# Moving the shifted bit pattern of some VectorE exponential groups to GpSimd, in seven pieces each

## The chip, the cores and the metric

The kernel runs on one core of one Trainium2 chip. The metric is the device time of one launch in microseconds (us). The engines are called by the names of the profile: PE is TensorE (matmuls; PEld are its weight loads), ACT is ScalarE, DVE is VectorE, POOL is GpSimd, and SP issues the DMAs. In the profile L1227 means line 1227 of the kernel.

## The reference

A layer norm of `x` (2048 tokens of 512 features) feeds two branches, whose results are added to `x`: an attention of 32 heads of 16 features each, and a gated linear unit with 1792 hidden features.

```python
qkv = (xn @ wqkv).reshape(B, S, 3, H, Dh)            # H = 32, Dh = 16
scores = jnp.einsum("bhqd,bhkd->bhqk", q, k) * (Dh ** -0.5)
p = softmax(scores)
A = jnp.einsum("bhqk,bhkd->bhqd", p, v).reshape(B, S, D) @ wo
gate, up = xn @ W_gate, xn @ W_up
Bo = (gate * (gate > 0) * up) @ W_down
return x + A + Bo
```

The softmax needs 32 x 2048 x 2048 exponentials. They are the largest part of the work outside the matmuls, and the change is in how some of them are made.

## The kernel before

**Blocks, groups, units.** The attention is cut into 32 blocks: four stretches of 512 queries (`c4`), four groups of heads (`gg`) and two halves (`ee`). A block covers four heads at a time, and has 16 groups, one for each stretch of 128 keys (`kt`). A group is four score tiles of 128 keys by 512 queries, one for each of the four heads. A score tile is a matmul at L1195 into a PSUM bank.

**Two ways to an exponential.** Most groups go to ACT, in units of three and two tiles in turn (L1262): one `Exp` activation from PSUM into a ring in SBUF. 108 groups go to DVE instead. The table `D_POS` says which positions of each block they take. There `dve_exp` builds the exponential from bit patterns. Four passes (named d1, L1211) turn a score tile in PSUM into the 16-bit pattern of a power of two, each 512 columns of the tile `tp`. From `tp` come three more tiles of 128 x 2048: `tm` (d2 at L1222 and d5, a product, at L1226), `tn` (d3, L1224) and `ts_`, which is the pattern of `tp` with the integer 36 added (d4, L1227). The sum of the four, with weights that are put into copies of V, stands for the exponential; so a DVE group has four PV matmuls for each head (L1171, `pv_group`) where an ACT group has one. The tiles `tp`, `tn`, `tm` and `ts_` lie in `dring`, a ring with `NDR` = 9 slots of 2048 columns.

**PV.** The PV matmuls of a block accumulate in one PSUM bank. Apart from the first and the last of a block their order is free (`PV_FREE`). After the last one the bank is copied out (L1105), the sums go by DMA to POOL, which forms the reciprocals (L1123), these come back by DMA, and POOL multiplies the block's output by them in four pieces (L1133).

**Other work in the same loop.** Projections, the gated linear unit and the output projection use the matmul at L728, whose results leave PSUM through DVE passes at L780, L811, L935, L939 and L976.

**What sets the order.** Nothing runs as a loop on the chip. The kernel records each operation with an engine, a planned duration, a priority and its tiles (`Graph.op`); `Graph.run` then places all of them by list scheduling, gives out buffer slots as it goes, and so fixes one order for each engine's queue; `emit` writes the queues with semaphore waits. Two rules of `run` matter here. Operations with `lock=True` on DVE and POOL are not placed on top of each other. And an operation named `pm` on POOL is placed only beside a DVE operation that isn't locked, after the DVE operation before that one has ended; that end becomes a real wait, and the piece has to fit into the host's time with at most `SLIP` = 100 ns over. The DVE operations from PSUM are not locked; d2, d3, d4 and d5 are. Before the change only the four multiplies at L1133 are named `pm`.

Of the kernel before, what the change touches and what calls it, by code (L numbers as in the profile page):

```python
# [9 lines left out]
U16 = mybir.dt.uint16  # L10
FP16 = mybir.dt.float16
ACTF = mybir.ActivationFunctionType
ALU = mybir.AluOpType
# [19 lines left out]
NWS = 3  # L33
NQ = 3
NDR = 9
KD = (1, 5, 9, 13)
D_LEAD = 10.0
D_POS = (
    (), (2, 3, 8, 11), (2, 8, 11, 15), (6, 9, 10),
    (2, 4, 12), (1, 3, 9, 14), (5, 10, 15), (2, 3, 10, 11),  # L40
    (1, 5, 15), (3, 4, 5, 8), (5, 9, 15), (2, 3, 7, 13),
    (3, 4, 10), (2, 4, 9, 11), (2, 7, 12), (4, 9, 10, 14),
    (7, 10, 11), (1, 8, 9, 10), (6, 7, 11, 12), (3, 5, 11),
    (1, 8, 12, 14), (4, 8, 14), (8, 12, 15), (2, 7, 13, 15),
    (1, 8, 14), (3, 4, 11), (1, 6, 10, 13), (1, 7, 12),
    (1, 8, 9), (1, 8, 11), (1, 2, 6, 12), (1, 2, 8, 9),
# [26 lines left out]
SHIFT = 36  # L73
# [379 lines left out]
def bass_parallel_sum__mha_block__glu_gated_reglu__prompt_kernel(  # L453
# [16 lines left out]
    with ExitStack() as es:  # L470
        def sb(name, shape, dt):
            return es.enter_context(nc.sbuf_tensor(name, shape, dt))
# [27 lines left out]
        ring = sb("ring", [128, NRING * 5, 512], BF16)  # L500
        dring = sb("dring", [128, NDR, 4 * 512], BF16)
        vd = sb("vd", [128, len(KD), 2, H, VW], BF16)
        hT = sb("hT", [128, FT, 512], BF16)
# [12 lines left out]
        G = Graph()  # L516
        P_sc = Pool("sc", 2)
        P_b = Pool("b", 3)
        P_ring = [Pool("ring%d" % i, NRING) for i in range(2)]
        P_dr = Pool("dr", NDR)  # L520
        P_xn = Pool("xn", 4)
# [18 lines left out]
             reads=[t_pid], writes=[t_pid], prio=-890)  # L540
        G.op("DVE", 100, lambda e: e.tensor_scalar(hmask[:, 1:2], pid[:, 0:1], 1.0 / 16.0, None, op0=ALU.mult),
             reads=[t_pid], writes=[t_mask], prio=-889)
        G.op("DVE", 100, lambda e: e.tensor_scalar(hmask[:, 0:1], pid[:, 0:1], -1.0 / 16.0, 1.0, op0=ALU.mult, op1=ALU.add),
             reads=[t_pid], writes=[t_mask0], prio=-888)
# [4 lines left out]
             reads=[t_id], writes=[t_id], prio=-898)  # L549
# [9 lines left out]
             reads=[t_id32], writes=[t_id32], prio=60)  # L559
# [13 lines left out]
        for i in range(2):  # L573
            dma(lambda e, i=i: e.dma_start(q_scr[i, :, DH:2 * DH, :], qT[:, 0, :]), 128,
                reads=[t_qt0], writes=[t_qz[i]], prio=-600)
# [35 lines left out]
        for j in range(4):  # L611
            for ee in range(2):
                dma(lambda e, j=j, ee=ee: e.dma_start(Wo_p[32 * j:32 * j + DH, ee, :], wo_src[NGG - 1, j, ee, :, :]), 16,
                    reads=[t_woz], writes=[Tile()], prio=40)
# [198 lines left out]
        def proj_v(kt, prio, allowed=(1,)):  # L813
# [7 lines left out]
            else:  # L821
                G.op("DVE", 610, lambda e: e.tensor_copy(v_aug[:, kt, :, 0:DH], bank_of(t).rearrange("p (h d) -> p h d", h=H)),
                     reads=[t], writes=[tv], prio=prio)
            if kt in KD:
                i = KD.index(kt)
                tvd = t_vd[kt] = Tile("vd")
# [6 lines left out]
        blocks = [(c4, gg, ee) for c4 in range(NB) for gg in range(NGG) for ee in range(2)]  # L833
        order, on_dve = [], set()
        for blk, cuts in zip(blocks, D_POS):
            kts = list(KD) if blk != blocks[0] else [13, 9]
            take = sorted(cuts)
            mine = [kt for kt in range(NT) if kt not in kts[:len(take)]]
            seq = []
# [6 lines left out]
                seq.append(kt)  # L846
            order.append(seq)
        groups = [blk + (kt,) for blk, seq in zip(blocks, order) for kt in seq]
        units, at_group, cur = [], {}, []
        for g in groups:  # L850
            at_group[g] = len(units) + 0.0
# [299 lines left out]
        def pv_group(key, kt, u):  # L1151
# [9 lines left out]
            for k in range(ways):  # L1161
# [5 lines left out]
                def pv(e, k=k):  # L1167
                    ins = None
                    for j in range(4):
                        v = v_aug[:, kt, 8 * gg + 2 * j + ee, 0:VN] if k < 2 else vd[:, KD.index(kt), k - 2, 8 * gg + 2 * j + ee, 0:VN]  # L1170
                        ins = e.matmul(ps_b[32 * j:32 * j + VN, 0, :], v, src[j][1](k), start=(first and k == 0),  # L1171
# [21 lines left out]
        def score(e, bank, t):  # L1193
            c4, gg, ee, kt, j = t
            return e.matmul(bank, kT[32 * j:32 * j + 32, gg, 128 * kt:128 * kt + 128],  # L1195
                            qm[32 * j:32 * j + 32, t_q[(c4, gg)].slot, ee, :], start=True, stop=True, tile_position=(32 * j, 0))
# [3 lines left out]
        def dve_exp(g, u):  # L1200

            tp, tm, tn, ts_ = (Tile("dr", P_dr) for _ in range(4))
            t4 = [g + (j,) for j in range(4)]
            prev_d, mine = list(last_d), []
            for j, t in enumerate(t4):
                ts = Tile("ds", P_b, D_BANKS)
                G.op("PE", 225, lambda e, t=t, ts=ts: score(e, ps_b[:, ts.slot, :], t), mode="row", rows=(j,), reads=[t_q[t[:2]], t_k[(t[1], t[3] // 4)], t_kfirst] + ([t_q1] if t[:3] == (0, 0, 1) else []), writes=[ts],
                     prio=u + D_WAIT, name="dsc", after=u - D_AHEAD, order=prev_d if D_SEQ else ())
                G.ops[-1].acq.append(tp)
                mine.append(G.ops[-1])  # L1210
                o = G.op("DVE", 610, lambda e, j=j, ts=ts: e.tensor_scalar(dring[:, tp.slot, 512 * j:512 * j + 512].bitcast(U16), ps_b[:, ts.slot, :],  # L1211
                                                                    0.25 * LOG2E * 128.0, 128.0 * (127.0 - LOG2_SUM), op0=ALU.mult, op1=ALU.add),
                         reads=[ts], writes=[tp], prio=u - 960, name="d1")
                for w in tp.w[:-1]:
                    o.deps.pop(w, None)
                if tp in o.acq:
                    o.acq.remove(tp)
            last_d[:] = mine

            def b(t, dt=BF16):  # L1220
                return dring[:, t.slot, :].bitcast(dt) if dt is not BF16 else dring[:, t.slot, :]
            G.op("DVE", 600, lambda e: e.tensor_scalar(b(tm, U16), b(tp, U16), 0xFF80, None, op0=ALU.bitwise_or),  # L1222
                 reads=[tp], writes=[tm], prio=u - 3, name="d2", lock=True)
            G.op("DVE", 600, lambda e: e.tensor_scalar(b(tn, U16), b(tp, U16), 0xFF80, 1, op0=ALU.bitwise_and, op1=ALU.bitwise_or),  # L1224
                 reads=[tp], writes=[tn], prio=u - 2.5, name="d3", lock=True)
            G.op("DVE", 1140, lambda e: e.tensor_tensor(b(tm), b(tp), b(tm, I16), ALU.mult), reads=[tm, tp], writes=[tm], prio=u - 3, name="d5", lock=True)  # L1226
            G.op("DVE", 600, lambda e: e.tensor_scalar(b(ts_, U16), b(tp, U16), float(SHIFT), None, op0=ALU.add),  # L1227
                 reads=[tp], writes=[ts_], prio=u - 2.4, name="d4", lock=True)
            for i in range(4):
                where[g + (i,)] = ((tp, tn, tm, ts_), lambda k, i=i: dring[:, (tp, tn, tm, ts_)[k].slot, 512 * i:512 * i + 512])  # L1230

# [2 lines left out]
        for u, cl in enumerate(units):  # L1234
# [5 lines left out]
            n = len(cl)  # L1240
            while dve_todo and dve_todo[0][0] <= u:
                dve_exp(dve_todo.pop(0)[1], u)
# [24 lines left out]
            while pv_next < len(groups) and all(groups[pv_next] + (j,) in where for j in range(4)):  # L1267
                g = groups[pv_next]
# [4 lines left out]
        for i in range(4):  # L1273
# [26 lines left out]
            if i not in FIN_PE:  # L1300
                G.op("DVE", 610, lambda e, i=i, to_=to_, tz=tz: e.tensor_tensor(xn_sb[:, to_.slot, :], bank_of(tz), resid(i), ALU.add),
                     reads=[tz, t_res[m]], writes=[to_], prio=NU + 10 + i)
            else:
                G.op("ACT", 600, lambda e, to_=to_, tz=tz: e.activation(xn_sb[:, to_.slot, :], bank_of(tz), ACTF.Copy),
                     reads=[tz], writes=[to_], prio=NU + 10 + i)
            dma(lambda e, m=m, to_=to_: e.dma_start(out2[128 * m:128 * (m + 1), :], xn_sb[:, to_.slot, :]), 128, reads=[to_], writes=[Tile()],
                prio=NU + 10 + i, stream=("out", m % 8))
# [50 lines left out]
```

The softmax here doesn't subtract the row's maximum and nothing guards it: scores larger than these inputs give would overflow.

## Time and profile before

The time is 770.96 us, the median of 2 runs (770.05 to 771.87). The profiled run has a span of 772.3 us. The columns below are the groups of the page: total busy time of the group and the mean of one instruction.

| what | line | engine | count | busy us | mean ns |
|---|---|---|---|---|---|
| exponentials | L1262 | ACT | 647 | 739.4 | 1259 (two shapes mixed) |
| d1, PSUM to `tp` | L1211 | DVE | 432 | 289.6 | 684 |
| d5, product | L1226 | DVE | 108 | 131.2 | 1215 |
| d2 | L1222 | DVE | 108 | 73.9 | 686 |
| d3 | L1224 | DVE | 108 | 73.8 | 684 |
| reciprocals | L1123 | POOL | 30 | 95.0 | 3166 |

The page also draws the span in 40 equal slices, where 9 means busy for 90% or more of the slice:

```profile
DVE  8799999999999899999799999999999989999996
ACT  6999999999999999999799999999999999999995
POOL 3103012221213222121220122213012212221200
PEclk9999999999999999999799999999999999999999
```

Read down a column to see which engines are full at the same time. DVE and ACT are full nearly everywhere; POOL is mostly idle. The row PEclk is the clock that TensorE was granted, in tenths of full speed.

### The profile page before, as it was taken

How to read it: one execution, taken by the hardware profiler on the slowest of the kernel's cores; microseconds unless marked ns; L12 is line 12 of the kernel's file. 1: busy time of each engine (PE TensorE's matmuls, PEld its weight loads, DVE VectorE, ACT ScalarE, POOL GpSimd, SP SyncE). 2: the span in 40 equal slices, each digit the busy share in tenths (PEclk: the TensorE clock that was granted, in tenths of full speed). 3: DMA queues.
4: the chain of work that ended last, by engine and by line, in shares of the span. 5: the costliest groups of instructions: out<-in, count | busy, mean ns of one | idle time of the engine just before them, and what ended most of it. 6: DMA issues, size and time to landing. Idle time of an engine off the chain costs nothing.

```text
span 772.3 us, 21574 instructions
## 1 busy us (share of the span) xinstructions
PE 752.1 (97%) x9478; PEld 226.4 (29%) x9478; DVE 735.8 (95%) x1148; ACT 747.7 (97%) x662; POOL 159.8 (21%) x172
## 2 busy tenths in 40 slices
PE   8999999999999999999999999999999999999997
PEld 3322222222222322222223233222222322222323
DVE  8799999999999899999799999999999989999996
ACT  6999999999999999999799999999999999999995
POOL 3103012221213222121220122213012212221200
PEclk9999999999999999999799999999999999999999
DMA  7402221212111122222221122132310122231000
GB/s 224 136 12 65 55 59 28 71 43 73 48 31 42 58 75 56 57 68 71 51 62 37 43 71 70 46 82 71 79 48 23 55 65 77 66 91 37 23 24 33
DMA packets 95757, 46.83 MB, mean 61 GB/s; under 512 B 69936, under 2 KB 91824, under 8 KB 95664
## 3 DMA queue, kind: packets, MB, share of 16 engines
q1 hardware_dynamic: 95664, 45.46, 21.6%
q8 instruction: 74, 1.21, 0.6%
q14 instruction: 19, 0.16, 0.1%
HBM read 36.70 MB, written 8.50 MB: 59 GB/s over the span
## 4 chain that ended last, share of the span: by engine, by line
DVE 52%; PE 40%; ACT 6%; issue 1%; POOL 0%; DMA 0%; DVEq 0%
DVE dring L1211 19%; PE ps_b L728 15%; PE ps_b L1171 11%; PE ps_sc L1195 11%; DVE dring L1226 8%; ACT ring L1262 6%; DVE dring L1224 5%; DVE dring L1222 4%; DVE dring L1227 4%; DVE up_sb L935 3%; PE ps_b L1195 2%; DVE hT L939 2%; DVE Wv L1105 1%; DVE kT L811 1%; DVE stats L637 1%
## 5 line engine op out<-in xcount | busy, mean ns | idle before, releaser
L1262 ACT ACTIVATE ring<-ps_sc 128x1536 bf16<-128x1536 f32 (+1 forms) x647 | 739.4, 1259 | 8.7 <-PE ps_sc L1195 3.9
L1211 DVE TENSOR_SCALAR dring<-ps_b 128x512 uint16<-128x512 f32 x432 | 289.6, 684 | 15.0 <-PE ps_b L1195 14.2
L1195 PE MATMUL ps_sc<-qm,kT 32*128 32x512 bf16 x1616 | 261.0, 386 | 3.5 <-ACT ring L1262 2.2
L1195 PE MATMUL ps_b<-qm,kT 32*128 32x512 bf16 x432 | 164.0, 387 | 1.8 <-DVE dring L1211 1.2
L1171 PE MATMUL ps_b<-ring,v_aug 128*17 128x512 bf16 x1616 | 144.5, 384 | 3.4 <-DVE Wv L1105 2.4
L1123 POOL TENSOR_TENSOR rrec<-rsum,minus 128x16 f32<-128x16 f32 x30 | 95.0, 3166 | 177.4 <-DMA rsum<-Wv 177.3
L1226 DVE TENSOR_TENSOR dring<-dring 128x2048 bf16<-128x2048 bf16 x108 | 131.2, 1215 | 0.0
L1195 PEld LDWEIGHTS ps_sc<-qm,kT 32*128 32x128 bf16 x1616 | 61.9, 91 | 229.9 <-ACT ring L1262 202.2
L1133 POOL TENSOR_TENSOR x_sb<-Wv,rb 128x128 bf16<-128x128 f32 x100 | 45.6, 456 | 334.4 <-DVE dring L1226 98.7
L1171 PE MATMUL ps_b<-dring,vd 128*17 128x512 bf16 x864 | 80.3, 384 | 1.0 <-DVE dring L1226 0.5
L1171 PE MATMUL ps_b<-dring,v_aug 128*17 128x512 bf16 x864 | 80.2, 386 | 0.1
L1222 DVE TENSOR_SCALAR dring<-dring 128x2048 uint16<-128x2048 uint16 x108 | 73.9, 686 | 0.7
L1224 DVE TENSOR_SCALAR dring<-dring 128x2048 uint16<-128x2048 uint16 x108 | 73.8, 684 | 0.0
L1227 DVE TENSOR_SCALAR dring<-dring 128x2048 uint16<-128x2048 uint16 x108 | 73.2, 684 | 0.0
L728 PE MATMUL ps_b<-xnT,wus 128*32 128x512 bf16 x896 | 70.8, 392 | 0.8 <-DVE dring L1211 0.5
L728 PE MATMUL ps_b<-xnT,wgs 128*32 128x512 bf16 x896 | 69.3, 386 | 1.3 <-DVE up_sb L935 0.3
L1171 PEld LDWEIGHTS ps_b<-ring,v_aug 128*17 128x17 bf16 x1616 | 36.9, 89 | 59.9 <-issue 35.0
L1195 PEld LDWEIGHTS ps_b<-qm,kT 32*128 32x128 bf16 x432 | 38.7, 91 | 43.9 <-DVE dring L1211 26.2
L728 PE MATMUL ps_b<-Wd,hT 128*32 128x512 bf16 x672 | 50.3, 382 | 0.0
L935 DVE COPY up_sb<-ps_b 128x512 f32<-128x512 f32 x56 | 38.3, 684 | 1.9 <-PE ps_b L728 1.9
L1171 PEld LDWEIGHTS ps_b<-dring,vd 128*17 128x17 bf16 x864 | 20.5, 89 | 34.4 <-issue 10.6
L939 DVE SCALAR_TENSOR_TENSOR hT<-ps_b,up_sb 128x512 bf16<-128x512 f32 x42 | 28.7, 683 | 1.4 <-PE ps_b L728 1.4
(109 smaller groups left out, 373.7 us busy)
## 6 DMA issues: line engine op xcount, KB each, us to landing
rb<-rec_scr SPq DMA_DIRECT2D x30, 256.0 KB
wus<-in_B_W_up_dram SPq DMA_DIRECT2D x56, 128.0 KB, 2.7
wgs<-in_B_W_gate_dram SPq DMA_DIRECT2D x56, 128.0 KB, 2.4
qm<-q_scr SPq DMA_DIRECT2D x30, 128.0 KB
o_scr<-x_sb SPq DMA_DIRECT2D x25, 128.0 KB
q_scr<-qT SPq DMA_DIRECT2D x17, 128.0 KB
xr_sb<-in_A_x_dram SPq DMA_DIRECT2D x16, 128.0 KB, 2.4
out_dram<-xn_sb SPq DMA_DIRECT2D x16, 128.0 KB, 1.7
```

The lines of the kernel that those rows point to most:

```text
L728: ins = e.matmul(bank_of(tile, sub)[32 * j:32 * j + 32, :], st[:, 32 * j:32 * j + 32], mv, start=(i == 0), stop=(i == n - 1), tile_positio ...
L935: G.op("DVE", 610, lambda e: e.tensor_copy(up_sb[:, tup.slot, :], bank_of(tu)), reads=[tu], writes=[tup], prio=slots[1] + EV)
L1123: G.op("POOL", 3000, lambda e: e.tensor_tensor(rrec[:, par, :], rsum[:, par, :], minus[:, 0:1].to_broadcast([128, 16]), ALU.pow), reads=[t ...
L1133: o = G.op("POOL", 200 + 1080 // N_MUL, lambda e, a=w * k, b=w * k + w: e.tensor_tensor(oT_of(tn)[:, a:b], o_sb[:, to.slot, a:b], rb[:, tr ...
L1171: ins = e.matmul(ps_b[32 * j:32 * j + VN, 0, :], v, src[j][1](k), start=(first and k == 0), stop=(last and k == ways - 1), tile_position=( ...
L1195: return e.matmul(bank, kT[32 * j:32 * j + 32, gg, 128 * kt:128 * kt + 128], qm[32 * j:32 * j + 32, t_q[(c4, gg)].slot, ee, :], start=True ...
L1211: o = G.op("DVE", 610, lambda e, j=j, ts=ts: e.tensor_scalar(dring[:, tp.slot, 512 * j:512 * j + 512].bitcast(U16), ps_b[:, ts.slot, :], 0 ...
L1222: G.op("DVE", 600, lambda e: e.tensor_scalar(b(tm, U16), b(tp, U16), 0xFF80, None, op0=ALU.bitwise_or), reads=[tp], writes=[tm], prio=u - ...
L1224: G.op("DVE", 600, lambda e: e.tensor_scalar(b(tn, U16), b(tp, U16), 0xFF80, 1, op0=ALU.bitwise_and, op1=ALU.bitwise_or), reads=[tp], writ ...
L1226: G.op("DVE", 1140, lambda e: e.tensor_tensor(b(tm), b(tp), b(tm, I16), ALU.mult), reads=[tm, tp], writes=[tm], prio=u - 3, name="d5", loc ...
L1227: G.op("DVE", 600, lambda e: e.tensor_scalar(b(ts_, U16), b(tp, U16), float(SHIFT), None, op0=ALU.add), reads=[tp], writes=[ts_], prio=u - ...
L1262: return e.activation(ring[:, a:a + n, :], ps_sc[:, 3 * k0:3 * k0 + n, :], ACTF.Exp, scale=0.25)
```

## The change

For some of the 108 DVE groups the tile `ts_` is no longer made by one d4 pass on DVE, but on POOL. The new table `POOL_AT` names for each block the positions whose group does so, as far as they are positions of `D_POS`. The 2048 columns are cut into `N_ADD` = 7 pieces of 292 or 293 columns. Each piece is an operation named `pm` with `lock=True`, so the planner lays it beside a DVE pass that reads PSUM. The planned duration of a piece is 100 ns and `P_NS` = 1.4 ns for each column, its priority that which d4 had. The pieces wait for one another only in the queue's order, and the tile counts as written when the last one is done. `D_POS` is as it was, so the same 108 groups are on DVE. The purpose is to free DVE of these passes and to use time in which POOL is idle.

```diff
+N_ADD = 7
+P_NS = 1.4
+P_PRIO = -2.4
+POOL_AT = ((), (2,), (), (6,), (), (1,), (), (2,), (), (3,), (), (2,), (), (2,), (), (4,), (), (1,), (), (3,), (), (4,), (), (2,), (), (3,), (), (1,), (), (1,), (), (1,))
...
         groups = [blk + (kt,) for blk, seq in zip(blocks, order) for kt in seq]
+        on_pool = {blk + (seq[i],) for n, (blk, seq, cuts) in enumerate(zip(blocks, order, D_POS)) for i in POOL_AT[n] if i in cuts}
...
-            G.op("DVE", 600, lambda e: e.tensor_scalar(b(ts_, U16), b(tp, U16), float(SHIFT), None, op0=ALU.add),
-                 reads=[tp], writes=[ts_], prio=u - 2.4, name="d4", lock=True)
+            if g in on_pool:
+                cuts = [2048 * k // N_ADD for k in range(N_ADD + 1)]
+                for a, z in zip(cuts, cuts[1:]):
+                    o = G.op("POOL", 100 + int(P_NS * (z - a)), lambda e, a=a, z=z: e.tensor_scalar(b(ts_, U16)[:, a:z], b(tp, U16)[:, a:z], float(SHIFT), None, op0=ALU.add),
+                             reads=[tp], writes=[ts_] if a == 0 else [], prio=u + P_PRIO, name="pm", lock=True)
+                    if a:
+                        o.order.add(ts_.w[0])
+                        ts_.w.append(o)
+            else:
+                G.op("DVE", 600, lambda e: e.tensor_scalar(b(ts_, U16), b(tp, U16), float(SHIFT), None, op0=ALU.add),
+                     reads=[tp], writes=[ts_], prio=u - 2.4, name="d4", lock=True)
```

## The prediction

> **What bounds the kernel now.** I read the busy shares on the page first, then the windows by stage, then the groups of instructions, the waits, and a piece of the timeline.
>
> ```profile
> PE 752.1 (97%) x9478; PEld 226.4 (29%) x9478; DVE 735.8 (95%) x1148; ACT 747.7 (97%) x662; POOL 159.8 (21%) x172
> ```
>
> Three engines stand at 95 to 97%, so the shares alone do not say which one an edit on DVE (VectorE) would have to relieve. The windows do (columns: length, then busy us of PE, PEld, DVE, ACT, POOL, then the granted clock):
>
> ```profile
> 20.00:60.00 40.00, 38.41 (x511) 12.43 (x506) 33.53 (x64) 39.18 (x37) 5.83 (x5) 1.00 0.25 75
> 60.00:350.00 290.00, 284.15 (x3532) 82.69 (x3528) 286.65 (x435) 288.51 (x254) 63.12 (x66) 1.00 0.21 55
> 350.00:400.00 50.00, 48.80 (x583) 13.63 (x579) 45.71 (x69) 45.82 (x41) 9.67 (x10) 0.90 0.25 65
> 400.00:550.00 150.00, 148.46 (x1890) 44.26 (x1890) 147.34 (x223) 149.71 (x132) 32.37 (x31) 1.00 0.23 61
> 550.00:600.00 50.00, 48.67 (x578) 13.67 (x570) 49.17 (x76) 48.84 (x45) 9.71 (x10) 0.97 0.18 44
> 600.00:755.00 155.00, 154.48 (x2053) 46.66 (x2045) 146.96 (x219) 154.25 (x136) 32.06 (x34) 1.00 0.20 54
> ```
>
> ACT (ScalarE) is busy 99.5% or more from 60 to 350, 400 to 550 and 600 to 755 us, while DVE drops to 146.96 of 155 in the last of these and to 286.65 of 290 in the first. Over 20 to 755 us ACT is idle 735 − 726.31 = 8.7 us and DVE 735 − 709.36 = 25.6 us. Of ACT's 8.7 us, 4.2 lie in the window with clock 0.90 and 1.2 in that with 0.97: a PE clock dip, not DVE. The rest is 3.3 us. The exponentials that fill ACT take a steady time by shape, and wait for PE alone:
>
> ```profile
> L1262 ACT ACTIVATE ring<-ps_sc 128x1536 bf16<-128x1536 f32 x323 | 475.3, 1471 | 8.0 <-PE ps_sc L1195 3.6 <-PE ps_b L1195 2.9 <-PE ps_b L1171 0.5
> L1262 ACT ACTIVATE ring<-ps_sc 128x1024 bf16<-128x1024 f32 x323 | 338.8, 1049 | 0.7 <-PE ps_sc L1195 0.4 <-PE ps_b L1195 0.2
> ```
>
> So ACT is the bound, and the span could at best lose its 8.7 us: 771.0 − 8.7 = 762.3 us. The operation that is moved, and its present wait:
>
> ```profile
> L1227 DVE TENSOR_SCALAR dring<-dring 128x2048 uint16<-128x2048 uint16 x108 | 73.2, 684 | 0.0
> PEld ps_b L1171 <- DVE dring L1227: 8.8, 31, 0.5
> ```
>
> PE (TensorE) weight loads wait 8.8 us in all for the shifted tile; most of that is slack to an exponential still running. The nearest thing to the new pieces is the multiply of the normalisation on POOL (GpSimd), which the planner already lays inside PSUM passes:
>
> ```profile
> L1133 POOL TENSOR_TENSOR x_sb<-Wv,rb 128x128 bf16<-128x128 f32 x100 | 45.6, 456 | 334.4 <-DVE dring L1226 98.7 <-DVE dring L1211 71.3 <-DVE dring L1227 50.2
> 159.80 0.68 DVE L939 SCALAR_TENSOR_TENSOR hT<-ps_b,up_sb 128x512 bf16<-128x512 f32 x1
> ...
> 159.97 0.46 POOL L1133 TENSOR_TENSOR x_sb<-Wv,rb 128x128 bf16<-128x128 f32 x1 [8.37 <-DVE dring L1211]
> ...
> 160.40 1.22 DVE L1226 TENSOR_TENSOR dring<-dring 128x2048 bf16<-128x2048 bf16 x1
> ```
>
> The GpSimd piece starts 0.17 us after its host pass and ends at 160.43, 0.03 us after the next, two-port operation was issued; that one still came at the ordinary 0.60 us spacing. Over the timeline, of 118 such pieces inside PSUM passes, 48 are followed by an all-SBUF operation; start offset median 162 ns, host spacing 601 ns, and three of the 48 hosts show 716.
>
> **What the Trainium skill says.** "SBUF — State Buffer", section "Who interferes with whom": GpSimd shares a port pair with VectorE as an exclusive lock; VectorE takes it in two-port modes or with two SBUF inputs, not with a PSUM source and at most one SBUF input. The trace agrees as far as it goes: the 601 ns spacings show undisturbed passes. "GPSIMD Engine Reference", section 3.1, gives about 1.03 cycles an element when port-bound and 1.8 for a good loop, at 1.2 GHz (0.86 and 1.5 ns). No row here has a one-input pass of this width to check it. "TensorE: Matmul & The Clock Gate", Part 1: the matmul clock is halved after a slack stretch, in free-running windows of 3413 ns. The trace agrees: 0.50 in every window from 372 to 382 us.
>
> **Part by part.** *Removed.* The new table has 16 entries, one in each odd block (I count 16 in the diff), always the first VectorE group of its block. So 16 L1227 operations leave DVE. Their issue spacing is 0.600 us, their 684 ns overlapping the next start: 16 × 0.600 = 9.6 us of DVE.
>
> *Added.* 16 × 7 = 112 pieces of 292 or 293 elements on POOL. Lower bound of one: the 128x4 TENSOR_SCALAR at L630 takes 228 ns, a memset of 512 elements at L554 takes 529 and one of one element 98, so 0.84 ns an element: 228 + 289 × 0.84 = 471 ns. Upper, an estimate from the skill's 1.8 cycles: 228 + 289 × 1.5 = 662 ns. The planner charges 510. I take 566, the middle. POOL then gains 112 × 0.566 = 63 us on 159.8: 223 us, far from bound.
>
> *Collisions.* A piece starts 162 ns into its host and ends at 728 ns; the next DVE operation would start at 601, so it overhangs 127 ns. An overhang of 18 ns costs nothing now, so about 109 ns is lost where the next operation needs the pair: 48/118 = 41% of 112, or 46 times: 5.0 us. Ends: 471 ns gives (162 + 471 − 601 − 18) = 14 ns × 46 = 0.6 us, 662 gives 205 × 46 = 9.4 us. DVE nets +9.6 − 5.0 = 4.6 us, between +0.2 and +9.0. It had 25.6 us of idle time, so even the worst end does not make it the bound.
>
> *Waits added.* Each piece waits for the DVE operation ahead of its host. Behind it in POOL's queue stand the other pieces, the reciprocal of L1123 (3.17 us) and the L1133 multiplies, whose DMA chain has most of a block. PV matmuls of the group wait for the last piece. Seven pieces need seven PSUM passes: about 630 passes in 740 us is 0.85 per us, so 8.2 us at least against 0.6 us now, 10 with normalisation pieces between. A block lasts some 753/32 = 23.5 us, a group 1.47; the moved group stands at position 1 to 6, so 9 or more groups (13 us) follow it, and its PV may be accumulated late: I cost this at nothing.
>
> *Buffers.* The source and shifted tiles keep 2 of 9 slots some 9 us longer, 16 times: 288 slot-us of 9 × 740 = 6660, 4%. New L1211 passes may start later there; the 12 exponential units in the ring hide it. Nothing again.
>
> *Order.* The program is list-scheduled as a whole, so every queue shifts a little. ACT's non-dip idle of 3.3 us can shrink by perhaps 1.5 us through earlier releases of PSUM banks (weight loads wait 26.2 us for L1211 now). Nothing on ACT is removed. Sum: 771.0 − 1.5 = 769.5 us.
>
> **The rivals.** *A, forecast (0.57):* ACT stays the bound, 763 to 773 us, centre 769.5.
>
> *B, small loss from order and clock (0.28):* late pieces or full slots leave PE stretches thin, and the clock dips more often. The dip at 372 us cost ACT 4.2 us and the one near 573 us 1.2; two more large ones less the 1.5 give 771 + 8.4 − 1.5 = 778 us. For it: two dips already occur and the order is planned with modelled times. Against: the 60 to 350 us stretch has none.
>
> *C, slower by over 2% (0.08):* a piece is far over its pass. At 1.0 us it would overhang 561 ns, reach over the next operation whatever it is, and so hold up a two-port one nearly every time: 112 × 0.54 = 60 us of DVE, less 9.6 freed and 25.6 idle: 25 us, 796 us. Against: the 471 to 662 ns bounds.
>
> *D, DVE is the bound after all (0.07):* all 9.6 us come through, 761.4. For it: DVE carries 52% of the chain of waits, and is nearly full from 60 to 250 us. Against: ACT was idle 8.7 us only, so the table of windows does not admit it in full.
>
> **How the numbers follow.** The likeliest case gives 769.5. The range takes A, most of D and most of B: 762.5 to 781, leaving C and the edges out. Faster by 2% needs 755.6, below ACT's floor of 762.3: 0.01. Slower by 2% is above 786.4: C and a tail of B, 0.08. Same: 0.91.
>
> **What would show it.** Right: L1227 has 92 instances, DVE busy time falls by 5 to 10 us, its idle time rises, ACT stays above 99% outside clock dips, a new POOL row of 112 takes 471 to 662 ns and lies in PSUM passes. Wrong: POOL rows above 700 ns, DVE spacings of 800 ns before L1222, L1224 or L1226, PE waits for POOL adding up to more than 5 us, or ACT idle time away from dips well over 3.3 us. It would also be wrong if ACT's busy time itself changed.

## The result, and the profile after

The kernel after takes 795.37 us (795.36 to 795.38, 2 runs) against 770.96 us before; the ratio is 1.0317, with a 95% interval of 1.0264 to 1.0369. It is 24.4 us slower, outside the range of the prediction. In the batches below the kernel before had a median of 770.0 to 770.1 us, and differences are taken from that: 25.3 us. Its single runs there lie between 768.4 and 774.5 us, the longer ones at a lower granted clock (0.990 at 774.1 us, 0.998 at 768.4). The ratios are taken over the single runs of both kernels, so they are not the quotients of the medians.

Below are the head of the page and the table by stage of the kernel after (columns as in the prediction's table; the changed lines have moved down in the file, d4 is now L1241, the pieces are L1235, the exponentials L1276, PV is L1176).

```profile
PE 760.1 (96%) x9518; PEld 229.3 (29%) x9518; DVE 733.8 (92%) x1132; ACT 750.7 (95%) x662; POOL 290.8 (37%) x284
...
20.00:60.00 40.00, 38.47 (x515) 12.34 (x509) 33.20 (x62) 38.51 (x36) 12.99 (x12) 1.00 0.25 74
60.00:350.00 290.00, 280.02 (x3463) 81.94 (x3459) 279.45 (x420) 282.91 (x249) 108.88 (x106) 1.00 0.20 54
350.00:400.00 50.00, 47.27 (x588) 13.29 (x579) 47.43 (x71) 47.05 (x41) 19.67 (x20) 0.97 0.25 63
400.00:550.00 150.00, 144.60 (x1819) 42.15 (x1811) 139.71 (x209) 144.10 (x127) 56.55 (x50) 0.99 0.21 56
550.00:600.00 50.00, 49.08 (x587) 14.69 (x585) 46.98 (x71) 49.33 (x44) 19.37 (x19) 1.00 0.23 59
600.00:755.00 155.00, 149.81 (x1919) 43.88 (x1916) 143.20 (x212) 147.56 (x130) 57.08 (x52) 0.99 0.20 54
```

ACT is idle 735 − 709.46 = 25.5 us between 20 and 755 us, where it was 8.7 before. The clock is not the cause: its mean over the profiled run is 0.994, where it was 0.990, and its lowest window 0.97, where it was 0.90. DVE is idle 735 − 689.96 = 45.0 us in place of 25.6; the 16 passes that it lost explain 9.6 us of that rise and not the rest, so it waits more too. The groups of the same kernel show for what:

```profile
L1276 ACT ACTIVATE ring<-ps_sc 128x1536 bf16<-128x1536 f32 x323 | 475.5, 1472 | 19.7 <-PE ps_sc L1200 6.6 <-PE ps_b L1200 5.4 <-PE ps_b L1176 4.8
L1241 DVE TENSOR_SCALAR dring<-dring 128x2048 uint16<-128x2048 uint16 x92 | 63.8, 699 | 1.1 <-PE ps_b L1176 0.6 <-PE ps_b L1200 0.5
L1235 POOL TENSOR_SCALAR dring<-dring 128x293 uint16<-128x293 uint16 x64 | 73.4, 1154 | 4.9 <-DVE dring L1231 1.5 <-DVE dring L1227 1.1 <-DVE Wv L1110 0.9
```

A piece, planned at 510 ns, takes 1154 ns in the mean. The line's own view gives the spread (min/median/max), and the waits (total us, times, longest) name who waited for it:

```profile
L1235 POOL TENSOR_SCALAR dring<-dring x112: 937/958/2272, 42.6 to 771.3; 128x293 uint16<-128x293 uint16 x64, 128x292 uint16<-128x292 uint16 x48
PEld ps_b L1176 <- POOL dring L1235: 11.2, 7, 2.2
PE ps_b L1176 <- POOL dring L1235: 8.8, 6, 1.9
```

The shortest piece, 937 ns, is longer than a whole PSUM pass (0.60 us from start to start), so no piece lies inside one. The two last lines are the same stops seen twice: seven of weight loads, 11.2 us in all, and six of the matmuls behind them. In the kernel before, PE's list of waits has no line with POOL. One such stop, in the timeline of the kernel after (start, length; in brackets the idle time before and who ended it):

```profile
485.25 2.53 POOL L1235 TENSOR_SCALAR dring<-dring 128x293 uint16<-128x293 uint16 x2
...
487.75 3.35 POOL L1128 TENSOR_TENSOR rrec<-rsum,minus 128x16 f32<-128x16 f32 x1
487.83 0.10 PEld L1176 LDWEIGHTS ps_b<-dring,vd 128*17 128x17 bf16 x4 [2.18 <-POOL dring L1235]
487.83 0.39 PE L1176 MATMUL ps_b<-dring,vd 128*17 128x512 bf16 x4 [1.88 <-POOL dring L1235]
...
489.02 0.39 PE L1200 MATMUL ps_sc<-qm,kT 32*128 32x512 bf16 x3
...
489.46 1.45 ACT L1276 ACTIVATE ring<-ps_sc 128x1536 bf16<-128x1536 f32 x1 [1.86 <-PE ps_b L1200]
```

Read it from the top: the last two pieces of a group end at 487.78; the PV matmul that needs the tile has held up PE's queue for 1.88 us; the scores behind it come at 489.02; and ACT, whose work has nothing to do with this tile, has been idle for 1.86 us.

### The profile page after: what moved, and what is told of

It is laid out like the page before. It is cut to its first block, busy times and chain, and to the rows that moved or that the text cites. A ratio compares the mean times of both kernels' runs of the same rounds, so it can differ in the third digit from the quotient of the medians.

```text
span 793.6 us, 21752 instructions
## 1 busy us (share of the span) xinstructions
PE 760.1 (96%) x9518; PEld 229.3 (29%) x9518; DVE 733.8 (92%) x1132; ACT 750.7 (95%) x662; POOL 290.8 (37%) x284
## 4 chain that ended last, share of the span: by engine, by line
DVE 46%; PE 42%; POOL 6%; ACT 4%; issue 1%; DMA 0%; DVEq 0%
DVE dring L1216 18%; PE ps_b L732 16%; PE ps_b L1176 12%; PE ps_sc L1200 11%; DVE dring L1231 7%; POOL dring L1235 5%; DVE dring L1227 5%; DVE dring L1229 4%; ACT ring L1276 4%; DVE dring L1241 3%; DVE up_sb L940 2%; PE ps_b L1200 2%; DVE hT L944 2%; DVE Wv L1110 1%; POOL rrec L1128 1%
## 5 line engine op out<-in xcount | busy, mean ns | idle before, releaser
L1276 ACT ACTIVATE ring<-ps_sc 128x1536 bf16<-128x1536 f32 (+1 forms) x647 | 742.3, 1260 | 26.0 <-PE ps_b L1200 7.9
L1200 PE MATMUL ps_b<-qm,kT 32*128 32x512 bf16 x432 | 162.0, 386 | 4.7 <-DVE dring L1216 1.5
L1235 POOL TENSOR_SCALAR dring<-dring 128x293 uint16<-128x293 uint16 (+1 forms) x112 | 126.1, 1148 | 86.8 <-DVE dring L1216 22.0
L1176 PE MATMUL ps_b<-ring,v_aug 128*17 128x512 bf16 x1616 | 143.7, 383 | 3.3 <-DVE Wv L1110 2.0
L1231 DVE TENSOR_TENSOR dring<-dring 128x2048 bf16<-128x2048 bf16 x108 | 131.5, 1219 | 0.0
L1128 POOL TENSOR_TENSOR rrec<-rsum,minus 128x16 f32<-128x16 f32 x30 | 99.4, 3314 | 76.0 <-DMA rsum<-Wv 76.0
L1176 PE MATMUL ps_b<-dring,vd 128*17 128x512 bf16 x864 | 80.0, 382 | 9.9 <-POOL dring L1235 8.8
L1176 PE MATMUL ps_b<-dring,v_aug 128*17 128x512 bf16 x864 | 79.3, 381 | 1.0 <-DVE dring L1229 0.7
L1227 DVE TENSOR_SCALAR dring<-dring 128x2048 uint16<-128x2048 uint16 x108 | 76.0, 708 | 0.5
L1229 DVE TENSOR_SCALAR dring<-dring 128x2048 uint16<-128x2048 uint16 x108 | 75.5, 702 | 0.3 <-PE ps_b L1176 0.3
L1241 DVE TENSOR_SCALAR dring<-dring 128x2048 uint16<-128x2048 uint16 x92 | 63.8, 699 | 1.1 <-PE ps_b L1176 0.6
L1176 PEld LDWEIGHTS ps_b<-ring,v_aug 128*17 128x17 bf16 x1616 | 36.4, 89 | 63.2 <-issue 41.2
L1176 PEld LDWEIGHTS ps_b<-dring,vd 128*17 128x17 bf16 x864 | 20.5, 89 | 45.5 <-POOL dring L1235 11.2
```

The source lines that it names most:

```text
L1128: G.op("POOL", 3000, lambda e: e.tensor_tensor(rrec[:, par, :], rsum[:, par, :], minus[:, 0:1].to_broadcast([128, 16]), ALU.pow), reads=[t ...
L1235: o = G.op("POOL", 100 + int(P_NS * (z - a)), lambda e, a=a, z=z: e.tensor_scalar(b(ts_, U16)[:, a:z], b(tp, U16)[:, a:z], float(SHIFT), N ...
L1276: return e.activation(ring[:, a:a + n, :], ps_sc[:, 3 * k0:3 * k0 + n, :], ACTF.Exp, scale=0.25)
```

## The experiments

Three explanations stood against each other: the tile comes late and stops PE (1), long pieces hold up DVE's all-SBUF passes at the port pair (2), or the new order of the queues is worse in itself (3). In the first three of the runs below the planner is given what it is given in the kernel after, so the engine queues hold the same instructions in the same order, except as the edit says.

### Short pieces in the same order

```diff
-lambda e, a=a, z=z: e.tensor_scalar(b(ts_, U16)[:, a:z], b(tp, U16)[:, a:z], float(SHIFT), None, op0=ALU.add),
+lambda e, a=a // 2, z=z // 2: e.tensor_tensor(b(ts_, I32)[:, a:z], b(tp, I32)[:, a:z], k36[:, 0:1].to_broadcast([128, z - a]), ALU.add),
```

Two neighbouring 16-bit patterns are one 32-bit integer, and `k36` holds 36*65537, so both get their 36.

> The kernel after with one edit: each piece takes the same columns as half as many 32-bit integers, with a two-input integer add of 36*65537, so it has 146 elements where it had 293. Queues of PE, DVE, ACT and SP are the same, instruction by instruction, and POOL's order too. If the length of a piece (950 ns bare, planned 510) is the cause, by whichever way, the pieces take about 490 to 510 ns (146 elements at the two-input rate of the 128-element multiply that took 456 ns) and the time falls back to 768 to 774 us. If the new order of the queues is the cause, it stays at 790 to 796 us.

775.88 us, ratio 1.0067 (1.0041 to 1.0094). 19.5 of the 25.3 us are gone with the length of the pieces; 5.8 remain. That is a little over the 768 to 774 us that were expected. The piece was shorter even than expected, PE hardly waits for it, and no DVE pass is lengthened (d4 has its 684 ns again):

```profile
L1235 POOL TENSOR_TENSOR dring<-dring,k 128x146 int32<-128x146 int32 x80 | 34.2, 427 | 108.7 <-DVE dring L1216 36.5 <-DVE dring L1227 19.2 <-DVE dring L1229 17.5
L1241 DVE TENSOR_SCALAR dring<-dring 128x2048 uint16<-128x2048 uint16 x92 | 62.4, 684 | 0.6 <-PE ps_b L1176 0.6
...
PEld ps_b L1176 <- POOL dring L1235: 0.5, 2, 0.2
```

So the length explains most, but not which way it works, and not the rest.

### PV does not wait for the pieces

```diff
-where[g + (i,)] = (..., lambda k, i=i: dring[:, (tp, tn, tm, ts_)[k].slot, 512 * i:512 * i + 512])
+where[g + (i,)] = (..., lambda k, i=i: zmov if k == 3 and g in on_pool else dring[...])
 G.run()
+# the pieces are taken out of what the PV matmuls wait for
```

> The kernel after, with its long pieces at their places, but the PV matmuls of the shifted tile read a tile of zeros in place of it (the shifted part of the 16 groups is left out of the sum) and so don't wait for the pieces. DVE, ACT, POOL and SP queues are the same. Slots of the ring are still given on only when the pieces are done. If the late tile stops PE (theory 1), the time falls by the 12 us of ACT gaps that end with a group's last piece, or more: 775 to 783 us. If the pieces hold up the all-SBUF passes of DVE through the shared port pair (theory 2) or the order is worse (theory 3), it stays at 790 to 796 us.

782.86 us, ratio 1.0157 (1.0127 to 1.0187). The late tile costs 795.4 − 782.9 = 12.5 us, the largest part, and of the size of the 11.2 us for which the weight loads waited. The 7.0 us down to the short pieces' 775.9 have another cause.

### Nothing waits for the pieces

```diff
-e.tensor_scalar(b(ts_, U16)[:, a:z], b(tp, U16)[:, a:z], float(SHIFT), None, op0=ALU.add)
+e.tensor_scalar(junk[:, 0:z - a], ident[:, 0:1].bitcast(U16).to_broadcast([128, z - a]), float(SHIFT), None, op0=ALU.add)
+# PV as in the run above; no other engine waits for a piece, each piece waits for the one ahead
```

> As the kernel with no wait of PV, a step further: the long pieces stand at their places in POOL's queue and wait for the same VectorE operations, but read one constant column and write a scratch tile, so that neither PV matmuls nor the next user of a ring slot waits for them (the shifted part of the 16 groups is left out). Each also waits for the piece ahead of it. What is left of their effect is the port pair that POOL shares with VectorE, and the order. If the 7.0 us between the kernel with no wait (782.9) and the short pieces (775.9) come through the port pair, it stays at 780 to 784 us; if they come from ring slots given on late, it falls to 775 to 778.

781.06 us, ratio 1.0133 (1.0097 to 1.0169). So about 1.8 us of the 7.0 were waits for ring slots. This is the least certain of the differences, as the two kernels ran in different batches, but the four runs of each agree within 0.3 us, and the trace of the run above has one such stop, at the score matmul of a DVE group, which takes the slot for `tp`:

```profile
PE ps_b L1200 <- POOL dring L1235: 1.3, 1, 1.3
```

5.2 us remain although no other engine waits for a piece. (Their waits for one another, 10.2 us in all, are POOL's own, and a piece is as long as before, 959 ns in the median.) Nor does one wait for the work that stands behind the pieces in POOL's queue: the only waits for POOL in this trace are 2.1 us in the layer norm at the start, which the kernel before has too. What is left is DVE's all-SBUF passes, which are longer than the 684 to 686 ns that they take in the kernel before:

```profile
L1229 DVE TENSOR_SCALAR dring<-dring 128x2048 uint16<-128x2048 uint16 x108 | 76.3, 709 | 0.2 <-PE ps_b L1176 0.2
L1227 DVE TENSOR_SCALAR dring<-dring 128x2048 uint16<-128x2048 uint16 x108 | 75.6, 704 | 0.5
L1241 DVE TENSOR_SCALAR dring<-dring 128x2048 uint16<-128x2048 uint16 x92 | 63.7, 698 | 0.6 <-PE ps_b L1176 0.6
```

Added up over the trace, 45 all-SBUF passes (the products at L1231 included) are lengthened by more than 25 ns, by 7.4 us together; in the kernel after it is 33 passes and 6.2 us, with short pieces one, by 0.03 us. That is explanation 2, and it is of the size of the 5.2 us. How much of the lengthening reaches the end of the kernel isn't measured apart.

### The piece by itself

A kernel of its own has nothing but pieces, first alone, then beside DVE.

> A small kernel of its own: pieces on POOL of many widths and three types, first alone, then beside 24 back-to-back all-SBUF passes of DVE (128x2048, 16 bit), then beside 24 passes of DVE from PSUM. The attention and all else is left out; the output is the input. Alone, a 293-element 16-bit piece should take 940 to 960 ns as its shortest in the kernel after, if that was its bare length, with some 2.5 ns an element over some 220 ns; the 146-element 32-bit one about 500 ns. Beside all-SBUF passes, if the port pair is an exclusive lock, pieces or passes should be stretched by up to the length of the other; beside PSUM passes neither should.

The run's time says nothing; its groups do. The pieces at L29, L31 and L33 run alone; those at L34 (16 bits) and L35 (32 bits) run beside DVE, eight of each beside all-SBUF passes and eight beside PSUM passes:

```profile
L29 POOL TENSOR_SCALAR dst<-src 128x2048 uint16<-128x2048 uint16 x3 | 16.1, 5364 | 0.2
L29 POOL TENSOR_SCALAR dst<-src 128x293 uint16<-128x293 uint16 x3 | 2.9, 953 | 0.2
L31 POOL TENSOR_SCALAR dst<-src 128x293 bf16<-128x293 bf16 x3 | 2.9, 953 | 0.2
L29 POOL TENSOR_SCALAR dst<-src 128x4 uint16<-128x4 uint16 x3 | 0.7, 227 | 4.6 <-DMA va<-in_A_x_dram 4.4
L33 POOL TENSOR_TENSOR dst<-src,k 128x1024 int32<-128x1024 int32 x3 | 5.7, 1890 | 0.2
L33 POOL TENSOR_TENSOR dst<-src,k 128x146 int32<-128x146 int32 x3 | 1.3, 428 | 0.2
L35 POOL TENSOR_TENSOR dst<-src,k x16: 427/584/757, 91.7 to 110.3; 128x146 int32<-128x146 int32 x16
```

A 16-bit add costs 227 ns and then (5364 − 227)/2044 = 2.51 ns an element, the same for bf16. The 32-bit integer add costs (1890 − 428)/878 = 1.67 ns an element of twice the width, so a third of the other for the same bytes. Beside DVE, first all-SBUF and then PSUM passes, in two answers of the timeline (start, length of the run of instructions):

```profile
81.81 6.53 POOL L34 TENSOR_SCALAR dst<-src 128x293 uint16<-128x293 uint16 x4
82.20 5.04 DVE L85 TENSOR_SCALAR vb<-va 128x2048 uint16<-128x2048 uint16 x6
...
98.48 4.08 POOL L34 TENSOR_SCALAR dst<-src 128x293 uint16<-128x293 uint16 x4 [0.16 <-POOL dst L35]
98.68 3.67 DVE L89 TENSOR_SCALAR vb<-ps 128x512 uint16<-128x512 f32 x6
```

Beside all-SBUF passes four pieces take 6.53 us and six passes 5.04; beside PSUM passes 4.08 and 3.67. Single 16-bit pieces go from 957 to 1571 ns, and the passes from one start each 0.60 us to one each 0.83. Both sides pay for all-SBUF passes, and neither pays beside PSUM passes. The 32-bit pieces are stretched too, from 428 to 757 ns (the largest in the line of L35): they are not spared, they are only short enough, at 427 ns, to fit beside a PSUM pass of 0.60 us.

The Trainium skill ("SBUF — State Buffer", section "Who interferes with whom"), on which the prediction drew, says which pairs contend, and this run agrees with that. It also says that the engine that issues first blocks the other for its whole instruction. This run does not show that: two passes went by for each piece, which started each (6.53 − 1.57) / 3 = 1.65 us, and two passes and a piece one after the other would take 2 x 0.60 + 0.95 = 2.15 us. The measurement decides here: the two slow each other down, and neither is shut out for the other's whole length.

### Pieces at their true price

```diff
-N_ADD = 7
-P_NS = 1.4
+N_ADD = 18
+P_NS = 2.5
-o = G.op("POOL", 100 + int(P_NS * (z - a)), ...
+o = G.op("POOL", 228 + int(P_NS * (z - a)), ...
```

> The kernel after with 18 pieces of 113 or 114 elements in place of seven, planned at 228 ns + 2.5 ns an element (513 ns), so that the planned and real length should agree and a piece really lies inside a pass. It needs 18 passes a group, so a tile takes 20 us and more to form, and the plan knows it. If a wrong price of the piece is the cause, pieces take 490 to 540 ns, PE waits little for POOL, and the time is 768 to 778 us. If it is the use of POOL as such (slots of the ring kept longer, port pair), 785 us or more.

782.80 us, ratio 1.0170 (1.0127 to 1.0212): between what the two cases gave. The pieces now have their planned length (median 502 ns) and PE's weight loads wait 1.6 us in all for POOL. But a tile takes 18 passes to form, and 12.7 us are lost all the same. So with the right price the tile is no longer late for PE, but that alone does not save the change. Whether this loss is the long-held slots or again the order isn't separated here.

### The order alone

The 5.8 us that short pieces leave could be the pieces or the order. This kernel has nothing on POOL. It is the one before, with the planned duration of d4 changed for the same 16 groups.

```diff
-G.op("DVE", 600, lambda e: e.tensor_scalar(b(ts_, U16), ...
+G.op("DVE", 605 if g in moved else 600, lambda e: e.tensor_scalar(b(ts_, U16), ...
```

> The kernel before, with nothing on POOL; only the planned duration of d4 is 605 ns in place of 600 for the same 16 groups. The work of every engine is the kernel before's, instruction for instruction, but the list scheduler lays it in another order. Theory 3a (what is left of the loss with short pieces, 5.7 us, is the price of leaving an order that the positions of D_POS were fitted to): 774 to 779 us. Theory 3b (it is the pieces themselves, by slots of the ring kept longer or tiles that come late): 769 to 771 us.

777.26 us, ratio 1.0085 (1.0061 to 1.0109). The same instructions on every engine but for 92 more of PE's filler matmuls, and 7.1 us slower. ACT's waits in it and with the short pieces show the same kind of idle time, exponentials that wait for PV (first the kernel before, then the re-priced kernel, then the short pieces):

```profile
ACT ring L1262 <- PE ps_b L1171: 0.5, 1, 0.5
```

```profile
ACT ring L1262 <- PE ps_b L1171: 7.1, 7, 2.4
```

```profile
ACT ring L1276 <- PE ps_b L1176: 5.0, 7, 1.6
```

A second sample planned these passes at 620 ns.

> A second sample of an order alone: the kernel before with d4 of the 16 groups planned at 620 ns in place of 600, nothing on POOL. If leaving the fitted order costs some us whatever the cause, 772 to 778 us, and again not under 770.

773.09 us, ratio 1.0038 (1.0024 to 1.0051). Both orders are slower than the one before, by 3.1 and 7.1 us, and the 5.8 us lie between them. So a new order can cost that much without any piece on POOL. That the 5.8 us are only this, and not in part slots of the ring that the plan itself keeps longer, is likely but not shown.

### DVE relieved, with nothing put on POOL

```diff
-e.tensor_scalar(b(ts_, U16), b(tp, U16), float(SHIFT), None, op0=ALU.add)
+e.tensor_scalar(b(ts_, U16)[:, 0:w], b(tp, U16)[:, 0:w], float(SHIFT), None, op0=ALU.add)   # w = 2 for the 16 groups, and PV reads zeros for them
```

> The kernel before, in its own order, but d4 of the same 16 groups does 2 of its 2048 columns, and the PV matmuls read a tile of zeros in its place (the shifted part of these groups is left out). DVE is relieved of the 16 passes, with nothing put on POOL: the gain that the change is for, without its costs. If ACT is the bound, as the prediction held, DVE idles 8 to 10 us longer and the time is 768 to 771 us. If DVE sets the pace, 760 to 763 us.

771.26 us, ratio 0.9996 (0.9977 to 1.0014), at the upper end of the expected 768 to 771. In the order of the kernel before, DVE is freed of what the change is to free it of, and no gain shows. DVE's busy time falls from 735.8 to 728.3 us and ACT's stays:

```profile
PE 746.9 (97%) x9478; PEld 225.8 (29%) x9478; DVE 728.3 (95%) x1148; ACT 747.2 (97%) x662; POOL 159.6 (21%) x172
```

### The change done with what was learned, and its control

Six 32-bit pieces a group at their measured price, and new positions in `D_POS` and `POOL_AT` for the shortest plan (109 groups on DVE, 18 of them with POOL).

```diff
-N_ADD = 7
-P_NS = 1.4
+N_ADD = 6
+P_NS = 0.8325
-o = G.op("POOL", 100 + int(P_NS * (z - a)), ...
+o = G.op("POOL", 185 + int(P_NS * (z - a)), ...
+# D_POS and POOL_AT with other positions; pieces as in the first run
```

> The change done with what the runs have shown: pieces as 32-bit integer adds, six to a group, planned at their measured price (185 + 1.67 ns an element: 470 ns), and positions of VectorE groups and of POOL's groups searched anew for the shortest plan (109 groups on VectorE, 18 of them with POOL). If the order and the length of a piece were all that was wrong, 765 to 769 us, at or a little under the kernel before; if pieces cost something that the plan doesn't know, 772 us or more.

769.63 us, ratio 0.9989 (0.9976 to 1.0003), just over the expected 765 to 769. The whole 25 us are recovered, with more groups on POOL than the change had, and no more than that: it can't be told from the kernel before. The control is the kernel before with other positions and no POOL:

> The control to the kernel with new positions: the kernel before, without POOL, with its positions of VectorE groups searched anew in the same way and for as long (108 groups). The search found hardly anything here, so 768 to 772 us. If the search alone makes a kernel faster, it is as fast as the one with POOL.

771.44 us, ratio 1.0003 (0.9983 to 1.0023). It is a third new order, this one found by a search, and it is not slower. The intervals of the two overlap, so no gain from POOL is shown.

## Why the prediction was wrong

Taken apart in sequence, the 25.3 us are 12.5 for the tile that comes late, about 1.8 for slots given on late, 5.2 put down to the port pair, and 5.8 that stay with short pieces, which a new order alone can cost. (Each difference was taken with the others in place.) By the steps of the prediction:

- *Which engine is the bound.* That it is not DVE is shown: relieving DVE in the old order moved nothing. That it is ACT rests on the windows. In that order the change had nothing to gain, whatever a piece costs.
- *"Added", the price of a piece.* This is the term that failed. It was bounded by 471 and 662 ns and taken as 566; alone it measured 953, and 1148 in the kernel, over both widths. The fixed part, 228 ns from the 128x4 row, was right (227). The slope was not: a memset's 0.84 ns gave one end, and for the other the prediction took 1.5 ns from the 1.8 cycles of "GPSIMD Engine Reference", section 3.1, in the Trainium skill, which the page calls a best case. A best case is no upper end. The measured slope is 2.51 ns. Neither end was a measurement of this operation, so the bounds did not bound.
- *"Collisions".* The path was right: all-SBUF passes are held up. The 6.2 us in all come near the 5.0 written down, but by luck. With the measured length the overhang is not 109 ns but 496 (162 + 953 − 601 − 18), and 46 such cases would be 22.8 us; in the trace 33 passes were lengthened, by 0.19 us in the mean. And by that step only DVE's total counted; since DVE had idle time, the loss was set to come to nothing. In a fixed order a pass that is late is late for those behind it, and idle time elsewhere need not pay it back. By the runs it cost about 5.2 us.
- *"Waits added … I cost this at nothing."* This is the second step that failed: it cost 12.5 us, half of the loss. That PV may be accumulated in any order is a freedom of the planner. On the chip PE's queue is fixed, and the PV matmul stands where the planned 510 ns put it. The 13 us of later groups in the block were slack for the plan, not for the run. With the true price in the plan PE's wait was 1.6 us; with the true price in the prediction alone this step would still have stood at nothing.
- *"Buffers", nothing.* About 1.8 us.
- *"Order", a gain of 1.5 us.* No gain came. Two samples of an order alone lost 3.1 and 7.1 us. The positions in the table are probably fitted to one plan; a third order, with positions searched anew, lost nothing. Why an order costs what it does stays open.
- *Rival C* named a piece of 1.0 us and came to 796 us, near the 795.4 measured, but by 60 us of held-up DVE where the trace has 6.2. The piece was as it said; that the time came out too is luck. Its small chance rested on the bounds of the price.

Of the signs of being wrong that the prediction named, these came: pieces above 700 ns, more than 5 us of PE waiting for POOL, and more idle time of ACT.

## What to carry to other kernels

Before work is moved to another engine, time the operation in the very form and type that it will have there; a price taken from another operation does not bound it, and here a 32-bit view made the same work cost less than half. In a statically ordered program slack belongs to the planner and not to the chip: an operation that runs longer than planned stops the queue of whoever waits for it at its planned place, and an engine's total idle time did not absorb that here. And when a list scheduler's inputs were fitted to one order, measure what a mere reordering costs before a difference of one per cent is put down to an edit.

## What the runs showed of the hardware

All of this is from the kernel that has only pieces and passes. GpSimd's 16-bit `tensor_scalar` add was dear for one input: 2.51 ns an element, against 1.67 ns for a two-input 32-bit integer add that carries two of these elements. A GpSimd piece beside back-to-back all-SBUF passes is not shut out, and doesn't shut VectorE out: the 16-bit piece takes 1571 ns in place of 957, the 32-bit one 757 in place of 428, and a pass starts each 0.83 us in place of 0.60. Beside passes from PSUM, pieces and passes keep their 957 ns and 0.60 us.
